# One 512-column multiplication for a unit's normalisation, and a rounding of g moved from GpSimd to ScalarE

## The chip, the core and the metric

The kernel runs on one core of a Trainium2 chip. A core has a matrix engine (TensorE: PE, with its weight loads as PEld), a vector engine (VectorE: DVE), an engine for functions and copies (ScalarE: ACT), a general engine (GpSimd: POOL) and a queue that issues transfers (SyncE: SP). Each engine works through its own list in order and waits on semaphores for the others. Time is device microseconds (us) from the first to the last instruction of one execution, with what lies around it; a kernel's time is the median of several runs.

## What is computed

Linear attention with random features, then a feed-forward layer with `h - tanh(h)`. Inputs are 8 batches, 8 heads, 576 tokens, 64 columns a head; 128 features; the second part has 4608 tokens, 512 columns in and 2048 hidden.

```python
def phi(x):
    proj = einsum('bhsd,md->bhsm', x, omega)
    h = proj - sum(x * x, -1, keepdims=True) / 2
    h = h - max(h, -1, keepdims=True)
    return exp(h) / sqrt(m)
q_p, k_p = phi(q * scale), phi(k * scale)
kv = einsum('bhsm,bhsd->bhmd', k_p, v)
z = sum(k_p, axis=2)
x = einsum('bhsm,bhmd->bhsd', q_p, kv) / (einsum('bhsm,bhm->bhs', q_p, z)[..., None] + 1e-6)
h = x @ w_in            # x as 4608 x 512
out = (h - tanh(h)) @ w_out
```

## The kernel before

Float32 precision is kept by splitting: each factor of a large product is a high part (a copy rounded to fp32r) and a low part (the factor minus its high part), and three of the four partial products are added up in PSUM: high by high, high by low, low by high.

**Attention** comes in units. A k unit (batch b, head pair c) makes the sums over keys; a q unit (chunk ch of 256 tokens, head pair c) makes the rows of x for its tokens. There are 72 q units (18 chunks by 4 pairs). The first 12, of chunks 0 to 2, run in the mode `native`, the other 60 not. A q unit that isn't native goes through these steps: load; split into `qx` (L78, L132, L133); projection on PE (L145); copy and minimum (L146, L149); exponential on ACT (L153) into `phi_q`, four blocks of 128 columns; denominators `dn` by four reductions on DVE (L350) and a reciprocal (L353); the four blocks multiplied by their `dn` (L354 to L359); four transposes on PE into `pt` (L366); split into `qh` and `ql` (L384, L385); product `pn` (L391, L392); columns put into `later` (L396 to L399). When four units of a chunk are done, `x_split` makes the chunk's `xh` and `xl` (L404, L405).

The multiplication of the four blocks asks `bank("norm")` for an engine each time. Outside `native` the list is DVE, DVE, DVE, ACT, so the first three blocks are done by DVE (L359, 128x128 each) and the last by ACT (L357).

**The feed-forward layer** goes through chunks 0 and 1 together, then chunks 2 to 5 one by one (`ffn_h`, L468 to L475, and `ffn_out`, L486 to L488), then chunks 6 to 17 in six wide blocks of two chunks, 16 steps f each. A wide step (`wide_h`) makes h for 128 hidden columns and 512 tokens by 12 matmuls (L529), tanh on ACT (L532), `g = h - tanh(h)` on DVE (L533), and then deals with the two halves of g apart. The first half is used at once: its high part `ge_w[:, 0]` by ACT (L534), its low part by DVE (L535), and six matmuls (L542 to L544, `po_w`). The second half is kept: its high part (L537) and its low part (L538), both by POOL, go into places of the weights that are no longer needed (`w`), and after the 16 steps they are the left factors of the `last` matmuls. The tile `g_w` can be written again when all four have read it.

**Order.** The program is written as interleaved generators (`tick`, `beat`), by tables of starting times, and a scheduler in the tile framework then sets the order of each engine's list by a timing model of its own, so a change of an instruction can move others. In the first 200 us of the trace chunks 0 to 2 and the decoding of weights run, until 437 us the chunks up to 5 with the attention of the next, until 870 us the wide blocks with the rest of the attention (block 0 begins around 437 us), and after that wide blocks with hardly any attention.

Of the kernel before, what the change touches and what calls it, by code (L numbers as in the profile page):

```python
# [14 lines left out]
ALU = mybir.AluOpType  # L15
AX = mybir.AxisListType

B, H, S, D, M = 8, 8, 576, 64, 128
NT, DM, DFF = B * S, H * D, 2048
P = 128  # L20
# [14 lines left out]
def favor_attention_ffn(ctx: ExitStack, tc: tile.TileContext, qT, kT, va, vt, omT, w, out):  # L35
# [12 lines left out]
    nc = tc.nc  # L48
# [18 lines left out]
    def bank(kind):  # L67
        tags = mode[kind]
        tags.append(tags.pop(0))
        return tags[-1]  # L70
# [19 lines left out]
    junk = const.tile([P, M], F32, name="junk")  # L90
# [44 lines left out]
    def features(lhs, name):  # L135

        n = len(lhs)
        ph = att("phi", [P, 4, M], F32, f"phi_{name}")
        nb = sb.tile([P, 4], F32, tag="nb", name=f"nb_{name}", bufs=12)

        for g in range(0, n, 2):
            m = min(2, n - g)
            pj = ps.tile([P, 2, 2 * M], F32, tag=bank("pj"), name=f"pj_{name}_{g}")
            for i in range(m):
                nc.tensor.matmul(pj[:, i], lhs[g + i], om2, start=True, stop=True)  # L145
            nc.scalar.copy(ph[:, g : g + m], pj[:, :m, M:])  # L146
            for i in range(m):
                j = g + i
                nc.vector.tensor_tensor_reduce(  # L149
                    ph[:, j], pj[:, i, :M], ph[:, j], scale=-SCALE, scalar=3.0e38,  # L150
                    op0=ALU.add, op1=ALU.min, accum_out=nb[:, j : j + 1])
        for j in range(n):
            nc.scalar.activation(ph[:, j], ph[:, j], AF.Exp, bias=nb[:, j : j + 1], scale=-1.0)  # L153
        return ph

    def features_f(f, toks, name):

        n = 2 * len(toks)
        ph = att("phi", [P, 4, M], F32, f"phi_{name}")
        nb = sb.tile([P, 4], F32, tag="nb", name=f"nb_{name}", bufs=12)  # L160
        pj = ps.tile([P, 4, M], F32, tag=bank("pj"), name=f"pj_{name}")
        for i, (a, b) in enumerate(toks):
            nc.tensor.matmul(pj[:, 2 * i : 2 * i + 2].rearrange("p a m -> p (a m)"), f[:, a:b],
                             om_bd.rearrange("p a m -> p (a m)"), start=True, stop=True)
        nc.vector.tensor_reduce(nb[:, :n], pj[:, :n], axis=AX.X, op=ALU.min)
        for j in range(n):
            nc.scalar.activation(ph[:, j], pj[:, j], AF.Exp, bias=nb[:, j : j + 1], scale=-1.0)
        return ph
# [150 lines left out]
    def q_unit(ch, c):  # L319
# [5 lines left out]
        while t < t0 + TC:  # L325
            e = min((t // S + 1) * S, t0 + TC)
# [3 lines left out]
        native = mode["native"]  # L330
        load(f, qT[c, :, t0 : t0 + TC])
        yield
        if native:
            ph = features_f(f, [(0, P), (P, 2 * P)], f"q{n}")
            ix = lambda h, t: 2 * t + h
        else:
# [3 lines left out]
            ph = features([x[:, h, t * P : (t + 1) * P] for h in range(2) for t in range(2)], f"q{n}")  # L340
            ix = lambda h, t: 2 * h + t
        dn = sb.tile([P, 4], F32, tag="dn", name=f"dn_{n}", bufs=8)
        for h in range(2):
            for t in range(2):
                i = ix(h, t)
                for b, s, e in pieces:
                    s, e = max(s, t * P), min(e, (t + 1) * P)
                    if s < e:
# [2 lines left out]
                            bank("junk")[r], ph[r, i], kvs[b, c][1][r, h], scale=1.0, scalar=EPS,  # L351
                            op0=ALU.mult, op1=ALU.add, accum_out=dn[r, i : i + 1])
        nc.vector.reciprocal(dn, dn)  # L353
        for i in range(4):  # L354
            e = bank("norm")
            if e is nc.scalar:
                e.mul(ph[:, i], ph[:, i], dn[:, i : i + 1])  # L357
            else:
                e.tensor_scalar(ph[:, i], ph[:, i], dn[:, i : i + 1], 1.0, op0=ALU.mult, op1=ALU.mult)  # L359
        yield  # L360
        if not native:
            yield
# [95 lines left out]
    def ffn_h(ch, s):  # L458

        p = ps.tile([P, 2, TC], F32, tag=bank("h"), name=f"h_{ch}_{s}")  # L460
        for j in range(1 if ch == 0 else 2):
            f = s if ch == 0 else 2 * s + j
            o = p if ch == 0 else p[:, j]
            r = slice(0, 2) if ch == 0 else ch % 2
            prods = [(wt[f][:, i, c * P : (c + 1) * P], x[:, r, c]) for c in range(NC)
                     for i, x in ((0, xh), (0, xl), (1, xh))]
            for i, (w_, x) in enumerate(prods):
                nc.tensor.matmul(o, w_, x, start=i == 0, stop=i == len(prods) - 1)  # L468
        g = sb.tile([P, 2, TC], F32, tag="g", name=f"g_{ch}_{s}")
        gh = sb.tile([P, 2, TC], F32R, tag="gh", name=f"gh_{ch}_{s}", bufs=2)  # L470
        gl = sb.tile([P, 2, TC], F32R, tag="gl", name=f"gl_{ch}_{s}", bufs=2)
        nc.scalar.activation(g, p, AF.Tanh)
        nc.vector.tensor_sub(g, p, g)  # L473
        nc.scalar.copy(gh, g)
        nc.vector.tensor_sub(gl, g, gh.bitcast(F32))  # L475
        return gh, gl
# [41 lines left out]
    def w_in(a, f, i, c):  # L518
        if a == 0:
            return wt[f][:, i, c * P : (c + 1) * P]  # L520
        j = TC + c % 2 * P
        return wt[2 * (f % NB) + c // 2][:, i, j : j + P]

    def wide_h(a, f):
        p = ps.tile([P, 2, TC], F32, tag=bank("h"), name=f"h_w{a}_{f}")
        prods = [(w_in(a, f, i, c), x[:, 0:2, c]) for c in range(NC)
                 for i, x in ((0, xh), (0, xl), (1, xh))]
        for i, (w_, x) in enumerate(prods):
            nc.tensor.matmul(p, w_, x, start=i == 0, stop=i == len(prods) - 1)  # L529
        g = sb.tile([P, 2, TC], F32, tag=bank("o"), name=f"g_w{a}_{f}", bufs=1 if mode["o"][-1] == "g" else 2)  # L530
        e = sb.tile([P, 2, TC], F32R, tag="gh", name=f"ge_w{a}_{f}", bufs=2)
        nc.scalar.activation(g, p, AF.Tanh)  # L532
        nc.vector.tensor_sub(g, p, g)  # L533
        nc.scalar.copy(e[:, 0], g[:, 0])  # L534
        nc.vector.tensor_sub(e[:, 1], g[:, 0], e[:, 0].bitcast(F32))  # L535
        hi, lo = [wt[f][:, i, 0:TC] for i in range(2)]
        nc.gpsimd.tensor_copy(hi, g[:, 1])  # L537
        nc.gpsimd.tensor_sub(lo, g[:, 1], hi.bitcast(F32))  # L538
        return a, f, e[:, 0], e[:, 1]

# [18 lines left out]
    def tick(new=(), force=False):  # L559
# [10 lines left out]
        chain=True, kvw=(sb, 6), zb=(sb, 6), zb0=(a0, 4), phi=(a0, 8), ph5=(a0, 2), qf=(a0, 2), qt=(a0, 2),  # L570
        kf=(a0, 3), native=True, junk=[junk, a0.tile([P, M], F32, name="junk1")],
        norm=[nc.vector,nc.scalar], o=["gl", "gh"], pj=["pj0", "pj1", "po0", "po1"], pk=["pk", "h0"],
# [26 lines left out]
    while decoded < NF:  # L599
# [24 lines left out]
    kvf.clear()  # L624
    ak = open_pool("ak")
    mode.update(
        chain=False, native=False, norm=[nc.vector, nc.vector, nc.vector, nc.scalar], junk=[junk],
        hi=nc.scalar, pj=["pj0"], pk=["pk"], pt=["pj0"],
        phi=(ak, 3), qh=(ak, 1), ql=(ak, 1), kf=(ak, 1), kx=(ak, 1), qf=(ak, 1),
        qx=(ak, 1), vr=(ak, 1), khl=(ak, 2), vhl=(ak, 2), zs=(ak, 1), c1=(ak, 1), kvs=(ak, 1))  # L630
# [44 lines left out]
    for ch in range(2, C0):  # L675
# [5 lines left out]
        for s in range(NS):  # L681
            if s > 0 and ch + 1 not in split and xdone.get(ch + 1) == NC:
                x_of(ch + 1)
            g = (ch, s, *ffn_h(ch, s))
# [30 lines left out]
    for a in range(NL):  # L715
# [3 lines left out]
        for f in range(NF):  # L719
            g = wide_h(a, f)  # L720
# [3 lines left out]
            i = NF * a + f + 6  # L724
# [7 lines left out]
        for i in range(2):  # L732
            p = ps.tile([P, DM], F32, tag=bank("h"), name=f"last_{a}_{i}")
# [44 lines left out]
```

## Time and profile before

| | |
|---|---|
| median of three runs | 1074.26 us (1074.21 to 1074.97) |
| the profiled execution | 1074.58 us |
| its span, first to last instruction | 1072.4 us |
| busy: PE, DVE, ACT, POOL | 1039.7, 857.9, 694.4, 440.2 us |
| mean granted TensorE clock | 0.995 |

A matmul of 512 columns is shown with 394 ns, but its end is modelled and the next starts some 0.23 us after it, so "busy" overstates how much PE does. A group of instructions is a line of the kernel with its engine, operation, tiles (out<-in), shape and count, then the busy time and the mean of one, then the idle time of the engine just before, with who ended it.

### The profile page before, as it was taken

The numbers are of one execution on the slowest core, as the hardware profiler recorded it, in microseconds if no ns is written. First come the engines' busy times: TensorE is split into PE (matmuls) and PEld (weight loads), VectorE is DVE, ScalarE is ACT, GpSimd is POOL, SyncE is SP. The second block draws the span as 40 slices with busy tenths as digits, with TensorE's granted clock in tenths as the row PEclk, the third lists the DMA queues.
The fourth block names the chain that finished last, engine by engine and source line by source line (L and its number), as shares of the span: only waits on it lengthen the run. The fifth ranks groups of instructions, "written<-read, shape, count | busy, mean of one in ns | idle before, by whom it ended". The sixth has DMA issues, their size and how long they took to land.

```text
span 1072.4 us, 19097 instructions
## 1 busy us (share of the span) xinstructions
PE 1039.7 (97%) x5608; PEld 887.8 (83%) x5608; DVE 857.9 (80%) x3010; ACT 694.4 (65%) x1813; POOL 440.2 (41%) x745
## 2 busy tenths in 40 slices
PE   8988999999999999999999999999999999999998
PEld 7767888988988888787888888878888888888886
DVE  6999986899999999988989988898889958742220
ACT  6997656778777777676776676667677646532220
POOL 4534541344434323555545554556355402221320
PEclk9999999999999999899999999999999999999999
DMA  8953631111111111223243332443254314332301
GB/s 281 276 172 123 251 111 56 33 34 53 33 54 36 53 38 53 82 67 91 73 126 111 114 108 91 126 130 107 63 155 124 107 42 147 113 103 85 99 0 40
DMA packets 85959, 106.17 MB, mean 99 GB/s; under 512 B 17632, under 2 KB 67936, under 8 KB 83808
## 3 DMA queue, kind: packets, MB, share of 16 engines
q1 hardware_dynamic: 85776, 104.92, 31.2%
q8 instruction: 45, 0.74, 0.3%
q14 instruction: 58, 0.48, 0.1%
q10 hardware_dynamic: 80, 0.03, 0.0%
HBM read 87.10 MB, written 17.83 MB: 98 GB/s over the span
## 4 chain that ended last, share of the span: by engine, by line
PE 55%; DVE 30%; ACT 7%; issue 5%; DMA 1%; POOL 1%; SPq 0%; DVEq 0%; POOLq 0%; ACTq 0%
PE h_w L529 15%; PE h L468 7%; DVE junk L350 4%; PE last L543 3%; PE last L544 3%; PE last L542 3%; PE po_w L544 3%; PE po_w L542 2%; PE po_w L543 2%; DVE phi_q L359 2%; PE po L486 2%; PE po L487 2%; PE po L488 2%; DVE g_w L533 2%; DVE vhl L262 2%
## 5 line engine op out<-in xcount | busy, mean ns | idle before, releaser
L529 PE MATMUL h_w<-xh,w 128*128 128x512 f32 x768 | 254.0, 394 | 2.7 <-DVE g_w L533 2.7
L529 PEld LDWEIGHTS h_w<-xh,w 128*128 128x128 f32 x768 | 143.8, 189 | 30.9 <-DVE g_w L533 4.4
L468 PE MATMUL h<-xh,w 128*128 128x256 f32 (+1 forms) x640 | 146.8, 307 | 5.0 <-DVE g L473 3.3
L529 PE MATMUL h_w<-xl,w 128*128 128x512 f32 x384 | 150.7, 393 | 0.0
L537 POOL CAST w<-g_w 128x256 fp32r<-128x256 f32 x96 | 39.7, 415 | 221.6 <-DVE g_w L533 209.5
L468 PEld LDWEIGHTS h<-xh,w 128*128 128x128 f32 x640 | 107.4, 190 | 12.5 <-DVE g L473 4.1
L350 DVE CUSTOM_DVE_ANT_0 junk<-phi_q,zb 128x128 f32<-128x128 f32 (+1 forms) x320 | 105.3, 330 | 14.8 <-ACT phi_q L153 1.0
L533 DVE TENSOR_TENSOR g_w<-h_w,g_w 128x512 f32<-128x512 f32 x96 | 65.6, 685 | 58.0 <-ACT g_w L532 57.5
L468 PE MATMUL h<-xl,w 128*128 128x256 f32 (+1 forms) x320 | 98.0, 307 | 0.3 <-DVE xl L405 0.3
L532 ACT ACTIVATE g_w<-h_w 128x512 f32<-128x512 f32 x96 | 56.6, 592 | 54.8 <-PE h_w L529 52.3
L153 ACT ACTIVATE phi_q<-phi_q,nb_q 128x128 f32<-128x128 f32 x240 | 81.0, 393 | 16.8 <-DVE nb_q L149 15.7
L529 PEld LDWEIGHTS h_w<-xl,w 128*128 128x128 f32 x384 | 72.5, 189 | 12.8
L538 POOL TENSOR_TENSOR w<-g_w,w 128x256 fp32r<-128x256 f32 x96 | 79.5, 828 | 5.1
L437 POOL TENSOR_SCALAR a<-a 128x1024 f32<-128x1024 f32 x14 | 58.4, 4173 | 52.8 <-ACT a L433 28.0
L534 ACT CAST ge_w<-g_w 128x256 fp32r<-128x256 f32 x96 | 38.9, 406 | 59.6 <-DVE g_w L533 58.5
L542 PE MATMUL po_w<-w,ge_w 128*128 128x512 f32 x192 | 75.8, 395 | 0.3 <-ACT ge_w L534 0.3
L544 PE MATMUL last<-w 128*128 128x512 f32 x192 | 75.3, 392 | 0.0
L543 PE MATMUL last<-w 128*128 128x512 f32 x192 | 75.3, 392 | 0.0
L542 PE MATMUL last<-w 128*128 128x512 f32 x192 | 75.2, 392 | 0.0
L543 PE MATMUL po_w<-w,ge_w 128*128 128x512 f32 x192 | 75.2, 392 | 0.0
L253 POOL TENSOR_TENSOR khl<-phi_ka,khl 128x256 fp32r<-128x256 f32 x48 | 37.8, 791 | 85.1 <-DVE khl L252 78.3
L544 PE MATMUL po_w<-w,ge_w 128*128 128x512 f32 x192 | 70.7, 396 | 1.2 <-DVE ge_w L535 1.2
(173 smaller groups left out, 2914.3 us busy)
## 6 DMA issues: line engine op xcount, KB each, us to landing
w<-w_in SPq DMA_DIRECT2D x320, 128.0 KB, 2.4
raw<-w SPq DMA_DIRECT2D x16, 1024.0 KB, 7.8
kf<-kT SPq DMA_DIRECT2D x32, 288.0 KB, 3.1
qf<-qT SPq DMA_DIRECT2D x72, 128.0 KB, 2.1
out<-o SPq DMA_DIRECT2D x36, 256.0 KB, 2.2
w_in<-w SPq DMA_DIRECT2D x16, 512.0 KB, 3.4
v<-vt SPq DMA_DIRECT2D x24, 288.0 KB, 2.9
v<-va SPq DMA_DIRECT2D x8, 288.0 KB, 6.0
```

The costliest lines, as they stand in the source:

```text
L153: nc.scalar.activation(ph[:, j], ph[:, j], AF.Exp, bias=nb[:, j : j + 1], scale=-1.0)
L350: nc.vector.tensor_tensor_reduce(bank("junk")[r], ph[r, i], kvs[b, c][1][r, h], scale=1.0, scalar=EPS, op0=ALU.mult, op1=ALU.add, accum_ou ...
L437: engine.tensor_scalar(a.bitcast(F32), a.bitcast(F32), 2.0**-15, 122879.9921875, op0=ALU.max, op1=ALU.min)
L468: nc.tensor.matmul(o, w_, x, start=i == 0, stop=i == len(prods) - 1)
L529: nc.tensor.matmul(p, w_, x, start=i == 0, stop=i == len(prods) - 1)
L532: nc.scalar.activation(g, p, AF.Tanh)
L533: nc.vector.tensor_sub(g, p, g)
L537: nc.gpsimd.tensor_copy(hi, g[:, 1])
L538: nc.gpsimd.tensor_sub(lo, g[:, 1], hi.bitcast(F32))
L542: nc.tensor.matmul(o, h, wt[f][:, 0, DM:], start=f == 0, stop=False)
L543: nc.tensor.matmul(o, h, wt[f][:, 1, DM:], start=False, stop=False)
L544: nc.tensor.matmul(o, l, wt[f][:, 0, DM:], start=False, stop=f == NF - 1)
```

## The change

Two edits. Outside `native` a q unit's four blocks of 128 columns are multiplied by their `dn` in one DVE instruction of 512 columns, whose second operand is `dn` repeated along each block; ACT has no part in it. And in a wide step ACT rounds the kept half of g to its high part; POOL still makes the low part. Lines behind the multiplication stand three further down in the changed kernel (L537 becomes L540).

```diff
         nc.vector.reciprocal(dn, dn)
-        for i in range(4):
-            e = bank("norm")
-            if e is nc.scalar:
-                e.mul(ph[:, i], ph[:, i], dn[:, i : i + 1])
-            else:
-                e.tensor_scalar(ph[:, i], ph[:, i], dn[:, i : i + 1], 1.0, op0=ALU.mult, op1=ALU.mult)
+        if native:
+            for i in range(4):
...
+        else:
+            nc.vector.tensor_mul(ph, ph, dn.rearrange("p (i o) -> p i o", o=1).to_broadcast([P, 4, M]))
...
         hi, lo = [wt[f][:, i, 0:TC] for i in range(2)]
-        nc.gpsimd.tensor_copy(hi, g[:, 1])
+        nc.scalar.copy(hi, g[:, 1])
         nc.gpsimd.tensor_sub(lo, g[:, 1], hi.bitcast(F32))
...
-        chain=False, native=False, norm=[nc.vector, nc.vector, nc.vector, nc.scalar], junk=[junk],
+        chain=False, native=False, junk=[junk],
```

The scheduler's lists are the same up to the first q unit that isn't native, and differ in many places after it. Three places are shown.

ACT's list in wide block 2, around the end of step 7 and step 8 (`g_w2_7` and `g_w2_8` are their g, `phi_q13_0` belongs to the q unit of chunk 13, pair 0), before:

```order
L534 CAST ge_w2_7_9257<-g_w2_7_9256 128x256
L146 COPY phi_q13_0_9215<-pj_q13_0_2_9223 128x256
L78 CAST qx_13_1_9358<-qf_13_1_9313 64x256 x2
L153 ACTIVATE phi_q13_0_9215<-phi_q13_0_9215,nb_q13_0_9216 128x128 x4
L532 ACTIVATE g_w2_8_9291<-h_w2_8_9278 128x512
L357 ACTIVATE phi_q13_0_9215<-phi_q13_0_9215,dn_13_0_9233 128x128
L301 COPY c1_6_2_9176<-pk_6_2_8928 128x256
L396 COPY later_102<-pn_12_3_9179 64x256
L397 COPY later_102<-pn_12_3_9179 64x256
L534 CAST ge_w2_8_9292<-g_w2_8_9291 128x256
```

The same place in the changed kernel:

```order
L537 CAST ge_w2_7_9134<-g_w2_7_9133 128x256
L540 CAST w7_1078<-g_w2_7_9133 128x256
L146 COPY phi_q13_0_9095<-pj_q13_0_0_9097 128x256
L153 ACTIVATE phi_q13_0_9095<-phi_q13_0_9095,nb_q13_0_9096 128x128 x2
L387 CAST qh_12_3_9022<-pt_12_3_9017 128x512
L146 COPY phi_q13_0_9095<-pj_q13_0_2_9103 128x256
L78 CAST qx_13_1_9235<-qf_13_1_9190 64x256 x2
L535 ACTIVATE g_w2_8_9168<-h_w2_8_9155 128x512
L153 ACTIVATE phi_q13_0_9095<-phi_q13_0_9095,nb_q13_0_9096 128x128 x2
L301 COPY c1_6_2_9056<-pk_6_2_8811 128x256
L537 CAST ge_w2_8_9169<-g_w2_8_9168 128x256
L540 CAST w8_1133<-g_w2_8_9168 128x256
```

The multiplication by `dn`, which stood ahead of three copies and a cast, is gone, and the rounding of the kept half follows directly on the rounding of the other half in both steps.

POOL's list around step 7 of the same block, before:

```order
L537 CAST w7_1078<-g_w2_7_9256 128x256
L293 TENSOR_TENSOR zs_6_2_8929<-zs_6_2_8929,phi_km6_2_9010 64x128
L538 TENSOR_TENSOR w7_1078<-g_w2_7_9256,w7_1078 128x256
L261 CAST vhl_6_3_0_9385<-v_6_3_9276 128x2x64
L299 TENSOR_TENSOR zhl_6_2_9173<-zs_6_2_8929,zhl_6_2_9173 128x256
```

And in the changed kernel:

```order
L293 TENSOR_TENSOR zs_6_2_8812<-zs_6_2_8812,phi_km6_2_8893 64x128
L261 CAST vhl_6_3_0_9262<-v_6_3_9153 128x2x64
L541 TENSOR_TENSOR w7_1078<-g_w2_7_9133,w7_1078 128x256
L299 TENSOR_TENSOR zhl_6_2_9053<-zs_6_2_8812,zhl_6_2_9053 128x256
L261 CAST vhl_6_3_2_9268<-v_6_3_9153 128x2x64
```

POOL's one instruction of the step now comes after the cast of `v` (L261) that it stood ahead of.

DVE's list at the passage from chunk 5 to wide block 0, around 428 us of the trace (`phi_q8_0` is a unit of chunk 8, `ql_7_3` belongs to the last unit that block 0 needs), before:

```order
L302 TENSOR_TENSOR c1_4_0_5382<-pk_4_0_5069,c1_4_0_5382 128x256
L353 RECIPROCAL dn_8_0_5478<-dn_8_0_5478 128x4
L262 TENSOR_TENSOR vhl_4_1_2_5573<-v_4_1_5418,vhl_4_1_2_5573 128x2x64
L359 TENSOR_SCALAR phi_q8_0_5460<-phi_q8_0_5460,dn_8_0_5478 128x128 x3
L385 TENSOR_TENSOR ql_7_3_5302<-pt_7_3_5296,qh_7_3_5301 128x512
```

And in the changed kernel:

```order
L302 TENSOR_TENSOR c1_4_0_5322<-pk_4_0_5012,c1_4_0_5322 128x256
L353 RECIPROCAL dn_8_0_5418<-dn_8_0_5418 128x4
L262 TENSOR_TENSOR vhl_4_1_2_5510<-v_4_1_5358,vhl_4_1_2_5510 128x2x64
L388 TENSOR_TENSOR ql_7_3_5242<-pt_7_3_5236,qh_7_3_5241 128x512
L362 TENSOR_TENSOR phi_q8_0_5400<-phi_q8_0_5400,dn_8_0_5418 128x512
```

The subtraction that makes `ql_7_3` has changed places with the normalisation of chunk 8.

## Rows read from the trace of the kernel before

**Rows 1.** The page's part 4: shares of the chain that ended last.

```profile
PE 55%; DVE 30%; ACT 7%; issue 5%; DMA 1%; POOL 1%; SPq 0%; DVEq 0%; POOLq 0%; ACTq 0%
```

**Rows 2.** Stretches: from, to and length; each engine's busy time; clock; DMA.

```profile
core 0: us, PE busy (x) PEld busy (x) DVE busy (x) ACT busy (x) POOL busy (x), PEclk, DMA share, GB/s
...
200.00:437.00 237.00, 228.28 (x1510) 206.54 (x1509) 218.77 (x878) 179.71 (x490) 93.45 (x176) 0.99 0.14 42
437.00:870.00 433.00, 427.98 (x2214) 360.10 (x2214) 387.85 (x1470) 299.05 (x824) 222.03 (x416) 1.00 0.35 106
870.00:1072.40 202.40, 198.57 (x922) 165.34 (x920) 79.20 (x250) 70.05 (x166) 40.68 (x64) 1.00 0.25 79
```

**Rows 3.** Waits of PE between 437 and 870 us: total, times, longest.

```profile
PE h_w L529 <- DVE g_w L533: 2.7, 4, 1.3
PE po_w L544 <- DVE ge_w L535: 1.2, 3, 0.8
PE po_w L542 <- ACT ge_w L534: 0.3, 1, 0.3
```

**Rows 4.** Groups of instructions between 437 and 870 us.

```profile
L538 POOL TENSOR_TENSOR w<-g_w,w 128x256 fp32r<-128x256 f32 x64 | 52.1, 815 | 2.6
...
L535 DVE TENSOR_TENSOR ge_w<-g_w,ge_w 128x256 fp32r<-128x256 f32 x64 | 36.6, 573 | 5.4 <-ACT ge_w L534 4.9
...
L359 DVE TENSOR_SCALAR phi_q<-phi_q,dn 128x128 f32<-128x128 f32 x95 | 27.0, 341 | 0.7
L537 POOL CAST w<-g_w 128x256 fp32r<-128x256 f32 x64 | 26.4, 414 | 77.9 <-DVE g_w L533 77.1
...
L534 ACT CAST ge_w<-g_w 128x256 fp32r<-128x256 f32 x64 | 25.9, 406 | 41.1 <-DVE g_w L533 40.2
...
L357 ACT ACTIVATE phi_q<-phi_q,dn 128x128 f32<-128x128 f32 x32 | 12.9, 402 | 37.2 <-DVE dn L353 37.0
```

**Rows 5.** Groups of instructions between 200 and 437 us.

```profile
L475 DVE TENSOR_TENSOR gl<-g,gh 128x512 fp32r<-128x512 f32 x29 | 23.3, 804 | 3.0 <-ACT gh L474 2.7
...
L357 ACT ACTIVATE phi_q<-phi_q,dn 128x128 f32<-128x128 f32 x19 | 7.6, 402 | 4.0 <-DVE dn L353 4.0
```

**Rows 6.** Lines L535, L475 and L359: durations, shortest, median and longest (ns).

```profile
L535 DVE TENSOR_TENSOR ge_w<-g_w,ge_w x96: 390/426/1003, 444.6 to 1045.9; 128x256 fp32r<-128x256 f32 x96
...
L475 DVE TENSOR_TENSOR gl<-g,gh x48: 660/687/1528, 92.0 to 419.9; 128x512 fp32r<-128x512 f32 x48
...
L359 DVE TENSOR_SCALAR phi_q<-phi_q,dn x204: 269/281/1060, 32.1 to 938.6; 128x128 f32<-128x128 f32 x102
```

**Rows 7.** Timeline at 428 us, DVE, then ACT, then PE.

```profile
428.53 0.68 DVE L359 TENSOR_SCALAR phi_q<-phi_q,dn 128x128 f32<-128x128 f32 x3
429.12 0.68 DVE L385 TENSOR_TENSOR ql<-pt,qh 128x512 fp32r<-128x512 f32 x1
...
428.53 0.40 ACT L357 ACTIVATE phi_q<-phi_q,dn 128x128 f32<-128x128 f32 x1 [0.40 <-DVE dn L353]
...
431.05 0.37 ACT L396 COPY later<-pn 64x256 f32<-64x256 f32 x1
...
429.86 0.39 PE L391 MATMUL pn<-qh,kvw 128*128 128x256 f32 x1 [0.78 <-DVE ql L385]
...
432.74 0.77 PE L269 MATMUL pk<-khl,vhl 128*128 128x256 f32 x2 [1.47 <-POOL khl L253]
```

**Rows 8.** Busy time in stretches of 5 us around it, columns as in rows 2.

```profile
430.00:435.00 5.00, 3.46 (x16) 3.04 (x17) 4.13 (x18) 4.05 (x13) 3.05 (x7) 0.65 0.01 3
435.00:440.00 5.00, 5.00 (x22) 4.34 (x21) 4.68 (x19) 4.36 (x12) 2.23 (x7) 0.67 0.43 130
```

**Rows 9.** Timeline at 699 us, POOL, then DVE, then PE.

```profile
699.09 1.25 POOL L538 TENSOR_TENSOR w<-g_w,w 128x256 fp32r<-128x256 f32 x1
...
699.76 1.19 DVE L133 TENSOR_TENSOR kx<-kf,kx 64x576 fp32r<-64x576 f32 x1
...
702.09 0.73 PE L544 MATMUL po_w<-w,ge_w 128*128 128x512 f32 x2 [0.82 <-DVE ge_w L535]
```

More of the change, by code (lines that the diff above doesn't have):

```diff
@@ L353, in q_unit @@
         nc.vector.reciprocal(dn, dn)
-        for i in range(4):
-            e = bank("norm")
-            if e is nc.scalar:
-                e.mul(ph[:, i], ph[:, i], dn[:, i : i + 1])
-            else:
-                e.tensor_scalar(ph[:, i], ph[:, i], dn[:, i : i + 1], 1.0, op0=ALU.mult, op1=ALU.mult)
+        if native:
+            for i in range(4):
+                e = bank("norm")
+                if e is nc.scalar:
+                    e.mul(ph[:, i], ph[:, i], dn[:, i : i + 1])
+                else:
+                    e.tensor_scalar(ph[:, i], ph[:, i], dn[:, i : i + 1], 1.0, op0=ALU.mult, op1=ALU.mult)
+        else:
+            nc.vector.tensor_mul(ph, ph, dn.rearrange("p (i o) -> p i o", o=1).to_broadcast([P, 4, M]))
         yield
```

## The prediction, made before the changed kernel ran

> **What bounds the kernel now.** I read the chain of waits first, then busy time by stage, then who makes PE wait, then the groups of the lines that the change touches, and last the timeline at two places. The chain runs through PE for 55%, DVE for 30% and ACT for 7% [rows 1]. By stage, PE is busy all but 8.7 us of the 237 us from 200 to 437, all but 5.0 us of the 433 us of the wide blocks with attention, and all but 3.8 us of the last 202 us [rows 2]. DVE is second: 92% of the first of these stretches (218.77 of 237), 90% of the second (387.85 of 433), 39% of the last. So the kernel is bound by PE, and what can be won at all is where DVE's list, nearly full, makes PE wait. There is not much: the visible gaps are about 14 us in both stretches together, and one loss that isn't idle time: at 430 to 440 us the granted clock was 0.65 and 0.67 [rows 8], between 1.2 and 2.4 GHz on average, where PE stood idle for 0.78 and 1.47 us in short succession [rows 7]. That dip cost 0.35 x 5 + 0.33 x 5 = 3.4 us of full-speed PE.
>
> In the wide blocks the waits of PE are for DVE's two operations of a step, 2.7 us for g (L533) and 1.2 us for its low part (L535), and 0.3 us for ACT's rounding [rows 3]. Nothing there waits for POOL's L537 or L538, whose results are needed only after the block.
>
> **The multiplication, on DVE.** 60 units each lose three instructions of 128 columns and gain one of 512. Undisturbed, the three take 0.68 us from the first's start to the last's end, since the next starts while the one before is still ending, and a 512-column subtraction of DVE right behind takes 0.68 us too [rows 7]. So undisturbed the edit saves DVE nothing: four blocks now cost what three did, and the fourth is ACT's saving. Disturbed, the three cost 3 x (341 - 281) = 0.18 us more on average [rows 4, 6]; the nearest 512-column operation with both inputs in SBUF, L475, averages 804 ns where its median is 687, so 0.12 us more [rows 5, 6]. No row has an operand that is repeated along a block, as `dn` is now. The bounds are 60 x (0.12 - 0.18) = -3.6 us of DVE time, and 60 x 0.12 = +7.2 us if the new one is disturbed where the old ones were not; 30% of each on the chain is -1.1 to +2.2 us. I take **0**: the median rows are equal. The four transposes behind it now all wait for one end where the first could start after a third of it; the end is the same.
>
> The Trainium skill (VectorE: DVE Perf Modes, section The perf-mode tier table) says that float32 `tensor_scalar` in SBUF runs at twice the rate of `tensor_tensor`, which speaks against this edit: at the page's 0.96 GHz, 512 elements one by one against 384 two by two would be an estimated 0.33 us more a unit. The trace doesn't show that difference: 0.68 us against 0.68 us.
>
> **ACT.** It loses 60 multiplications (402 ns) and gains 96 casts, which I price at the identical shape that it does already, 406 ns [rows 4]. From 200 to 437 us that is only a gain: 19 instructions, 7.6 us, and the 4.0 us in which ACT stood at them waiting for the reciprocal [rows 5]. From 437 to 870 us it is 12.9 us less and 64 x 0.406 = 26.0 us more, a net 13.1 us; ACT goes from 299 to some 312 us of 433 and stays far from full. The cast adds no wait of its own: it waits for the same g as L534, and the order shows it directly behind L534. What queues behind it are copies of projections, exponentials and the next tanh, on which DVE waits. With ACT's 7% of the chain: +0.9 us for the net 13.1; -0.8 for the 11.6 us of the first stretch. In the second, 37.0 us of ACT's standing at L357 go as well [rows 4], with copies of `c1` and `later` behind it in the list; 7% is -2.6, of which I take half, -1.3, because what comes next often needs the same DVE. Sum **-1.2 us**; the bounds are -3.4 (relief whole, casts hidden) and +26 (each cast on the path).
>
> **POOL.** It loses 26.4 us (L537) in the second stretch. That time was idle cover anyway, POOL being half busy; what matters is DVE. L535 has a median of 426 ns and a longest of 1003 [rows 6], a mean of 573 in the stretch [rows 4]: 64 x 0.147 = 9.4 us of being held. One such chain is to be seen whole at 699 us: L538 runs for 1.25 us, DVE's L133 beside it for 1.19, L535 comes late and PE stands 0.82 us [rows 9]. Now L538 can't start until ACT has done two casts, 0.81 us after g, by which time an L535 that came promptly is nearly over. I take half of the 9.4 us as saved, and 30% of that for the chain: **-1.4 us**. The bounds are 0 and the waits of rows 3 whole, -4.2. On the other side L538 ends some 0.4 us later after g, and POOL's `khl` behind it with it; POOL is 1% of the chain [rows 1], so I cost that at nothing.
>
> The Trainium skill (SBUF — State Buffer, section Who interferes with whom) says that whichever of a GpSimd instruction and a DVE instruction with two SBUF inputs starts first holds the shared ports to its end. The stretched L133 agrees. By it L538's holding is not removed but moved on to whatever DVE does 0.4 us later, and this term could be 0.
>
> **The passage to block 0.** Here the order shows a real change: `ql_7_3` (L385) now precedes the multiplication, so it starts about 0.59 us earlier (428.53 for 429.12), and PE's wait of 0.78 us for it shrinks to about 0.2 [rows 7]. ACT loses L357 there (0.40 us, after a 0.40 us wait), so `later` (L396) comes earlier too. I take 0.6 + 0.4 = **-1.0 us**, and leave the clock as it was.
>
> **Sum.** 0 - 1.2 - 1.4 - 1.0 = -3.6 us. The profiled execution took 1074.58 us, so 1070.98; it stood 0.32 us over the median, which gives 1070.7 us. The last 202 us I cost at nothing: DVE and ACT have room there.
>
> **Rivals.**
>
> *No difference.* What is freed lies where PE sets the pace, or what held DVE holds it elsewhere; the passage alone remains. 1074.3 - 1.0 = 1073.3 us. For it: PE at 97 to 99% busy, and DVE's own work unchanged. Against: PE's waits in the wide blocks are for exactly those DVE operations.
>
> *Clock kept.* If the passage loses enough idle time, the clock doesn't fall at 431 us: 3.4 us more, 1067.3 us. For: two of its three gaps sit behind lists that moved (the third is `khl`, 1.47 us, and PE has transposes to do before it now). Against: the projections and short matmuls there remain.
>
> *Slower, through ACT.* Each cast delays what stands behind it by 0.406 us, 64 times in the second stretch. If the chain runs through ACT in a share s of the steps, the sum becomes -4.5 + 26 s; slower than the bound at s over a quarter, and at 0.4 it is +5.9, or 1080.2 us. For: ACT waits 40.2 us at L534 for g [rows 4], so it often arrives early and the cast then pushes all behind it. Against: ACT's 7% of the chain, and those very idle times as slack.
>
> *The multiplication is dearer.* If it takes L475's 804 ns against 680, DVE gets 7.2 us more and the time is 2.2 us above the forecast, 1072.9 us; that is within no difference. By the page's rates it would be 20 us of DVE and, at 30%, some 1077 us; rows 7 leave that little room.
>
> **Chances.** A measurement of this kernel tells about 0.2% (2.1 us) from no change, so faster means below 1072.1 us and slower above 1076.4. Forecast 0.46 (its own range 1068.5 to 1072.1); clock kept 0.15; no difference 0.25, with the dearer multiplication at 804 ns in it; slower 0.14, of which 0.02 for a multiplication at the page's rates. That makes faster 0.61, same 0.25, slower 0.14. The range goes from 1066.0, a little under the case of the kept clock for ACT's and POOL's better bounds, to 1077.0, leaving out most of the slower case.
>
> **What would show it.** Right: the new multiplication near 0.69 us when undisturbed; DVE's busy time within 10 us of before; L535's mean well under 573 ns; the cast at 406 ns; PE's waits for L533 and L535 below 3.9 us; L391's wait at the passage gone or small. Wrong: PE waits that end with ACT lines (L146, L532, L534), DVE idle time before L149 or L398 that grows by more than a few us; the L535 mean unchanged with other DVE lines stretched by L538; a second stretch at a low clock. An order that opens a new gap at a block's start, which no row of before can price, would make all of this wrong in either direction.

## The result, and the profile after

The changed kernel took 1079.40 us (median of 4 runs, 1078.47 to 1080.20) against 1074.62 us for the kernel before beside it: a ratio of 1.0044, 95% interval 1.0027 to 1.0061. The forecast was 1070.7 us, so the sign was wrong: 4.8 us slower instead of 3.6 us faster. The profiled execution took 1079.24 us, with a span of 1077.5 us against 1072.4.

In the code after, every line behind the first edit stands three lower: the cast `hi` is L540 (ScalarE now), the subtraction `lo` L541, `g` L536, the copy `ge` L537, its low part L538, and the new multiplication is L362.

Busy time (share of the span, instructions) and the chain that ended last, to be held against [rows 1]:

```profile
PE 1040.2 (97%) x5608; PEld 885.5 (82%) x5608; DVE 857.8 (80%) x2890; ACT 702.6 (65%) x1849; POOL 402.6 (37%) x649
...
PE 60%; DVE 27%; ACT 6%; issue 4%; POOL 2%; DMA 1%; DVEq 0%; SPq 0%; POOLq 0%; ACTq 0%
```

VectorE's work is the same to a tenth of a microsecond (857.9 before), GpSimd lost 37.6 us and ScalarE gained 8.2. Nothing became a bound by its amount of work. Against [rows 2]:

```profile
200.00:437.00 237.00, 227.40 (x1512) 204.49 (x1511) 219.22 (x830) 170.64 (x467) 91.40 (x169) 1.00 0.14 42
437.00:870.00 433.00, 423.79 (x2191) 355.49 (x2192) 382.67 (x1398) 306.48 (x851) 203.54 (x360) 1.00 0.35 104
...
870.00:1077.50 207.50, 203.68 (x949) 169.65 (x947) 84.90 (x256) 80.63 (x199) 24.74 (x32) 1.00 0.25 80
```

In the second row PE stands idle for 9.2 us where it was 5.0. Who makes it wait there, against [rows 3] (total us, times, longest):

```profile
PE h_w L532 <- DVE g_w L536: 4.6, 7, 1.0
PE po_w L547 <- DVE ge_w L538: 1.3, 2, 0.7
PE h_w L532 <- DVE xl L408: 0.8, 1, 0.8
PE pj_q L145 <- ACT g_w L535: 0.6, 1, 0.6
PE pt L369 <- DVE later L402: 0.6, 1, 0.6
PE pk L269 <- POOL khl L253: 0.6, 1, 0.6
```

The wait for `g` rose from 2.7 to 4.6 us, and four partners appear that were not in [rows 3]. The groups of the touched lines in the same stretch, against [rows 4]:

```profile
L541 POOL TENSOR_TENSOR w<-g_w,w 128x256 fp32r<-128x256 f32 x64 | 53.1, 832 | 76.3 <-ACT w L540 62.4 <-DVE nb_q L149 5.0 <-DVE dn L353 3.4
...
L538 DVE TENSOR_TENSOR ge_w<-g_w,ge_w 128x256 fp32r<-128x256 f32 x64 | 38.5, 603 | 5.1 <-ACT ge_w L537 4.4
...
L537 ACT CAST ge_w<-g_w 128x256 fp32r<-128x256 f32 x64 | 26.0, 407 | 42.7 <-DVE g_w L536 42.1
L540 ACT CAST w<-g_w 128x256 fp32r<-128x256 f32 x64 | 25.8, 403 | 1.4 <-DVE g_w L536 1.4
L362 DVE TENSOR_TENSOR phi_q<-phi_q,dn 128x512 f32<-128x512 f32 x31 | 24.5, 791 | 0.7
```

VectorE's subtraction for the low part (L538) was to become quicker than its 573 ns and became slower, 603. And at the passage to block 0, against [rows 7, 8], first the timeline, then two stretches of 5 us:

```profile
431.58 0.68 DVE L388 TENSOR_TENSOR ql<-pt,qh 128x512 fp32r<-128x512 f32 x1
432.18 0.68 DVE L362 TENSOR_TENSOR phi_q<-phi_q,dn 128x512 f32<-128x512 f32 x1
...
432.32 0.39 PE L394 MATMUL pn<-qh,kvw 128*128 128x256 f32 x1 [0.18 <-DVE ql L388]
```

```profile
430.00:435.00 5.00, 2.56 (x14) 1.65 (x13) 4.67 (x23) 3.13 (x11) 0.32 (x2) 1.00 0.23 76
435.00:440.00 5.00, 4.21 (x24) 3.10 (x23) 4.91 (x18) 4.60 (x15) 4.64 (x11) 1.00 0.11 35
```

Here the order did what the prediction read from it: the wait of 0.78 us is 0.18, and the granted clock stays at 1.00 where it was 0.65 and 0.67. So the condition of the rival *clock kept* was met, and the kernel is slower all the same.

### The profile page after: what moved, and what is told of

It reads as the page before. It is cut to its first block, busy times and chain, and to the rows that moved or that the text cites. A ratio compares the mean times of both kernels' runs of the same rounds, so it can differ in the third digit from the quotient of the medians.

```text
span 1077.5 us, 18913 instructions
## 1 busy us (share of the span) xinstructions
PE 1040.2 (97%) x5608; PEld 885.5 (82%) x5608; DVE 857.8 (80%) x2890; ACT 702.6 (65%) x1849; POOL 402.6 (37%) x649
## 4 chain that ended last, share of the span: by engine, by line
PE 60%; DVE 27%; ACT 6%; issue 4%; POOL 2%; DMA 1%; DVEq 0%; SPq 0%; POOLq 0%; ACTq 0%
PE h_w L532 16%; PE h L471 8%; PE last L545 4%; PE last L547 4%; PE last L546 4%; DVE junk L350 4%; PE po_w L547 3%; PE po_w L546 3%; PE po_w L545 3%; PE po L489 2%; PE po L490 2%; PE po L491 2%; DVE g_w L536 2%; PE pj_q L145 2%; DVE vhl L262 1%
## 5 line engine op out<-in xcount | busy, mean ns | idle before, releaser
L532 PE MATMUL h_w<-xh,w 128*128 128x512 f32 x768 | 250.5, 392 | 4.6 <-DVE g_w L536 4.6
L541 POOL TENSOR_TENSOR w<-g_w,w 128x256 fp32r<-128x256 f32 x96 | 77.8, 812 | 237.8 <-ACT w L540 212.0
L350 DVE CUSTOM_DVE_ANT_0 junk<-phi_q,zb 128x128 f32<-128x128 f32 (+1 forms) x320 | 103.1, 324 | 14.4 <-ACT phi_q L153 1.7
L536 DVE TENSOR_TENSOR g_w<-h_w,g_w 128x512 f32<-128x512 f32 x96 | 65.7, 686 | 55.1 <-ACT g_w L535 54.5
L153 ACT ACTIVATE phi_q<-phi_q,nb_q 128x128 f32<-128x128 f32 x240 | 82.3, 394 | 17.5 <-DVE nb_q L149 16.7
L535 ACT ACTIVATE g_w<-h_w 128x512 f32<-128x512 f32 x96 | 56.6, 593 | 52.6 <-PE h_w L532 48.9
L537 ACT CAST ge_w<-g_w 128x256 fp32r<-128x256 f32 x96 | 39.1, 407 | 67.5 <-DVE g_w L536 66.7
L538 DVE TENSOR_TENSOR ge_w<-g_w,ge_w 128x256 fp32r<-128x256 f32 x96 | 54.7, 571 | 15.9 <-ACT ge_w L537 15.0
```

What stands on the lines that cost most here:

```text
L350: nc.vector.tensor_tensor_reduce(bank("junk")[r], ph[r, i], kvs[b, c][1][r, h], scale=1.0, scalar=EPS, op0=ALU.mult, op1=ALU.add, accum_ou ...
```

## The experiments

Two questions were open after this: whether the two edits cost time as operations, or the scheduler's newly written lists do; and, if an edit does, through which engine. In the kernels whose lists are marked *of before* in the table, each engine's list of the kernel before is held fixed by a chain of order-only dependencies that is added at the kernel's end; in norm_new_order it is the list of the changed kernel. Only the named edit then differs.

```diff
+    for row in ORDER:                      # one list for each engine
...
+            if last is not None:
+                tc.add_manual_dep(ins[at], last.name, info, reason="order")
+            last = ins[at]
```

All ratios are to the kernel before on the same chip. The last three columns are us by which the profiled execution falls behind the profiled one of before: up to 98 us (the start), from there to 448 us (narrow chunks and the passage), and from there to the end. They are read from the start times of the same products of the up-projections, and are single executions. Where the lists differ, the last two columns depend on where the line is drawn: by the columns that have gone through PE, the changed kernel lies 2.7 us behind at 448 us, 1.1 at 500, 0.3 at 600 and 5.2 at 870, of which 1.1 are the start each time.

| kernel | operations | lists | ratio (95%) | start | to 448 | to the end |
|---|---|---|---|---|---|---|
| after | both edits | its own | 1.0044 (1.0027, 1.0061) | 1.1 | 1.6 | 2.4 |
| both_old_order | both edits | of before | 1.0028 (1.0017, 1.0040) | 1.4 | 0.5 | 2.3 |
| norm_new_order | multiplication | of after | 1.0013 (1.0003, 1.0022) | -0.5 | 1.1 | -0.5 |
| norm_only | multiplication | its own | 1.0051 (1.0038, 1.0064) | 1.2 | 1.6 | 3.9 |
| hi_only | hi on ScalarE | its own | 0.9991 (0.9982, 0.9999) | 1.3 | 0.2 | -1.1 |
| hi_old_order | hi on ScalarE | of before | 1.0022 (1.0013, 1.0031) | 0.3 | -0.2 | 3.3 |
| norm_old_order | multiplication | of before | 0.9990 (0.9981, 0.9998) | 0.4 | 0.1 | -1.2 |
| old_shift_a | as before | redrawn | 1.0035 (1.0022, 1.0047) | 1.3 | 1.5 | 0.9 |
| old_shift_b | as before | redrawn | 0.9992 (0.9983, 1.0001) | 1.4 | 2.4 | -1.8 |
| act_extra | + work on ScalarE | of before | 1.0030 (1.0018, 1.0043) | 2.0 | 0.0 | 3.6 |
| pool_short | - work on GpSimd | of before | 0.9975 (0.9964, 0.9986) | 0.5 | 0.1 | -1.8 |
| lo_late | hi on ScalarE, lo later | of before but lo | 1.0053 (1.0041, 1.0066) | 2.1 | 0.2 | 5.5 |
| hi_late | hi on ScalarE, later | of before but hi | 1.0026 (1.0017, 1.0035) | 0.5 | 0.1 | 3.1 |
| new_shift_a | both edits | redrawn | 1.0004 (0.9995, 1.0013) | 1.2 | 1.1 | -0.7 |
| new_shift_b | both edits | redrawn | 1.0008 (0.9999, 1.0017) | 0.7 | -1.5 | 2.9 |

### Operations or lists

Both edits in the lists of before, and the changed kernel's lists with GpSimd making `hi` again, directly ahead of `lo`:

> Both edits, but every engine's list is held to the order of the kernel before: the 512-column multiplication stands where the first of the three DVE multiplications stood, ACT's rounding of the kept half directly behind its rounding of the other half, and everything else as it was. Theory 'operations': ACT's 64 casts in the wide blocks with attention delay what DVE waits for, and the time is that of the changed kernel, 1077 to 1080 us. Theory 'lists': the operations are neutral or a small gain, as the prediction summed them, and the loss comes with the new lists that the scheduler made; then 1070 to 1075 us.

> The changed kernel's lists, but GpSimd makes the high part again, directly ahead of its low part in GpSimd's list; the 512-column multiplication stays. Theory 'operations': without ACT's casts the loss goes, 1072 to 1075 us. Theory 'lists': the lists are those of the changed kernel, so 1077 to 1080 us.

Then each edit alone, with the scheduler free:

> The 512-column multiplication alone, GpSimd makes the high part, the scheduler free to order. Theory 'operations': no ACT casts, so 1073 to 1075 us. Theory 'lists': a new order is drawn, and the time can lie anywhere from 1070 to 1081 us; nothing is said of the side.

> ACT's rounding of the kept half alone, the multiplication by the four separate instructions as before, the scheduler free to order. Theory 'operations': all of the loss, 1078 to 1081 us, or a little more since ACT keeps its 60 multiplications. Theory 'lists': a new order is drawn, anywhere from 1070 to 1081 us.

Measured: 1.0028, 1.0013, 1.0051, 0.9991. Neither theory fits all four. In fixed lists `hi` costs: taking it back in the lists of after brings 1.0044 to 1.0013. With the scheduler free it costs nothing (0.9991), and then the multiplication, which no list held fixed charges much for, is the slow one (1.0051). So each edit was also tried alone in the lists of before:

```diff
-        nc.gpsimd.tensor_copy(hi, g[:, 1])
+        nc.scalar.copy(hi, g[:, 1])
```

> The kernel before with one edit: ScalarE makes hi, right behind the copy of g's first half, and every engine's list is otherwise held to the order of the kernel before. Operations theory (ScalarE's cast delays what VectorE and TensorE wait for, whatever the order): of the 2.7 us that both edits cost in these lists (1.0028 of before) nearly all is this edit's, since taking it back in the changed kernel's lists gave about 3.3 us outside the start: 1.0020 to 1.0030 of before, the waits of h_w for g_w longer. Lists theory (both edits are neutral, the new lists lose): 0.998 to 1.001. Redraw theory (an edit of a fraction of a microsecond moves every later meeting of the engines, with either sign): anything between 0.998 and 1.003, and no simple sum with the other edit.

```diff
+            nc.vector.tensor_mul(ph, ph, dn.rearrange("p (i o) -> p i o", o=1).to_broadcast([P, 4, M]))
```

> The kernel before with the other edit: one multiplication of 512 columns at the place of the first of the four, every engine's list otherwise held to the order of the kernel before. Operations theory: the multiplication lasts as long as the three small ones together, so 0.999 to 1.001 of before. Lists theory: the same. Late-tile theory (the first transposes of a unit now wait for all four columns at once, and TensorE meets them sooner than VectorE ends): 1.001 to 1.003, with more waits of the transposes of phi_q on VectorE's multiplication. If this edit and the one of hi each cost 1 to 1.5 us, the 2.7 us of both in these lists are their plain sum.

Measured: `hi` 1.0022, the multiplication 0.9990. Three pairs share their lists and differ by `hi` alone: before to hi_old_order +0.22%, norm_old_order to both_old_order +0.38%, norm_new_order to after +0.31%. That is 2.4 to 4.1 us. Two pairs differ by the multiplication alone: -0.10% (before to norm_old_order) and +0.06% (hi_old_order to both_old_order). So the multiplication is neutral as an operation and `hi` is not.

### How much a redrawn list is worth

One number in the table of starts, and no operation, is changed, in the kernel before and in the changed one:

```diff
-                k = [(28,31,34,37),(43,46,49,52),(40,55,58,64),(61,70,76,82),(67,73,79,85)][ch - 3][c]
+                k = [(29,31,34,37),(43,46,49,52),(40,55,58,64),(61,70,76,82),(67,73,79,85)][ch - 3][c]
```

(the `_b` kernels turn 40 into 41 instead)

> The kernel before with no operation changed: one number in the table of starts, the first unit of the first wide chunk from 28 to 29, so that the scheduler writes other lists. Operations theory: the lists are of the same quality, so within 0.1% of before (0.999 to 1.001). Redraw theory: the time moves by 2 to 5 us, with either sign (0.995 to 1.005), which would be as much as the changed kernel lost.

> The kernel before with no operation changed: one other number in the table of starts, the first unit of the third wide chunk from 40 to 41. Operations theory: 0.999 to 1.001 of before. Redraw theory: 0.995 to 1.005, another value than that of the other shifted start. If both come out slower and neither faster, the lists of the kernel before are a picked draw: a change that redraws them pays some microseconds whatever it does.

> The changed kernel with no operation changed: the first unit of the first wide chunk starts at 29 instead of 28, so the scheduler writes other lists. If the changed kernel's own lists are an unlucky draw, this one comes out 1 to 4 us faster than it: 1.000 to 1.0035 of before. If the change itself asks for worse lists, 1.004 to 1.006.

> The changed kernel with no operation changed: the first unit of the third wide chunk starts at 41 instead of 40. Unlucky draw: 1.000 to 1.0035 of before, and another value than that of the other shifted start. Trait of the change: 1.004 to 1.006. With the operations alone at 1.0028 (both edits in the lists of the kernel before), draws on either side of that would say that the lists add spread and no cost of their own.

Measured: 1.0035 and 0.9992 around the kernel before, 1.0004 and 1.0008 around the changed one at 1.0044. The same operations span 0.4% by the draw of the lists, as much as the change was measured to cost. The changed kernel stands at the dear end of its own draws; what its lists lose beyond the other two is not a trait of the change. The three draws of before (1, 1.0035, 0.9992) average 1.0009 and those of the changed kernel 1.0019: with the scheduler free, these runs show no cost of the change that stands out from the spread.

### Through which engine `hi` costs

ScalarE's extra time and GpSimd's relief are now taken apart, both in the lists of before:

```diff
-        nc.scalar.copy(e[:, 0], g[:, 0])
+        nc.scalar.copy(e[:, 0], g[:, 0]); nc.scalar.copy(spare, g[:, 1, 0:16]); nc.scalar.copy(spare, g[:, 1, 16:32])
```

> The kernel before in its own lists, GpSimd keeping its cast of hi; ScalarE gets two more casts of 16 columns right behind the copy of g's first half, into a spare tile that nobody reads (together about as long as one of 256 columns, which left no room for a tile). ScalarE's-queue theory (the 0.4 us of the cast delay what stands behind it on ScalarE, and VectorE behind that): nearly the whole +2.4 us of the moved hi in these lists, 1.0015 to 1.003 of before. GpSimd's-subtraction theory (the cast costs ScalarE nothing that matters; it is lo, started a cast later, that meets VectorE's subtraction and holds up GpSimd's list): 0.999 to 1.001.

```diff
-        nc.gpsimd.tensor_copy(hi, g[:, 1])
+        nc.gpsimd.tensor_copy(hi[:, 0:16], g[:, 1, 0:16])
```

> The kernel before in its own lists, GpSimd's cast of hi cut from 256 to 16 columns (the other 240 columns of hi are left out: they keep the old weights, and lo is taken against those); ScalarE gets nothing. So GpSimd is relieved and nothing is added elsewhere. My prediction's term for VectorE's relief: 0.997 to 0.999 (some 1.4 us and more). GpSimd's-subtraction theory: the cast never held VectorE, and lo now starts earlier beside VectorE's subtraction of e, so VectorE's subtractions beside lo grow in number and the time is 0.999 to 1.001.

Measured: 1.0030 and 0.9975. The groups from 437 to 870 us that show the two edits, ScalarE's of act_extra, then GpSimd's of pool_short:

```profile
L534 ACT CAST spare<-g_w 128x16 fp32r<-128x16 f32 x128 | 25.9, 202 | 2.0
```

```profile
L537 POOL CAST w<-g_w 128x16 fp32r<-128x16 f32 x64 | 13.8, 217 | 80.0 <-DVE g_w L533 79.3
```

Two casts of 202 ns (25.9 us in the stretch, as the cast of 256 columns takes) cost 3.2 us with GpSimd untouched. ScalarE's-queue theory holds, GpSimd's-subtraction theory as the main cause falls. The relief of 0.2 us a step on GpSimd alone is worth 2.7 us, but not at the place where the prediction looked for it, VectorE's subtraction L535, whose mean was 573 ns before and is, in pool_short,

```profile
L535 DVE TENSOR_TENSOR ge_w<-g_w,ge_w 128x256 fp32r<-128x256 f32 x64 | 36.8, 575 | 5.4 <-ACT ge_w L534 4.9
```

The two effects' sum, +0.05%, is below the +0.22% of the moved `hi`, but the intervals (0.09 to 0.13% to either side each) don't settle whether the rest is real. What could be in it is that `lo` now waits for ScalarE.

VectorE's list is the same in these kernels, instruction for instruction, so its delay between 440 and 868 us can be split into longer waits and longer instructions. Act_extra falls 3.7 us behind there: waits that end with ScalarE grow by 1.6 us, waits that end with GpSimd by 0.9, and instructions by 1.1. Hi_old_order falls 3.7 us behind as well: 1.6, 0.8 and 1.5 (the rest are smaller waits and others). Pool_short gains 1.6 us: its instructions are 2.8 us shorter, and its waits 1.2 us longer. So the same cast time on ScalarE costs VectorE the same waits whether it is `hi` or work that nobody reads.

Two kernels moved one of the two steps in its list:

> ScalarE makes hi in the lists of the kernel before (1.0022 of before as it stood), but GpSimd's subtraction lo is moved behind the next item of GpSimd's list, in 56 of 96 places (in the others the next item is another lo). GpSimd's-subtraction theory (GpSimd stood waiting for ScalarE's cast with urgent work behind it): most of the 2.4 us come back, 0.999 to 1.0012. ScalarE's-queue theory: nothing comes back, 1.0015 to 1.003.

> ScalarE makes hi in the lists of the kernel before, but two places later in ScalarE's list, behind the next two items; GpSimd's list keeps lo in its place. ScalarE's-queue theory (the items right behind the cast are the ones that are late): a good part of the 2.4 us comes back, 0.999 to 1.0015. GpSimd's-subtraction theory: GpSimd waits for hi still longer, so 1.002 to 1.006.

Measured: 1.0053 and 1.0026; nothing came back in either. GpSimd's groups of lo_late, and then of hi_late, in the same stretch:

```profile
L538 POOL TENSOR_TENSOR w<-g_w,w 128x256 fp32r<-128x256 f32 x64 | 50.4, 787 | 30.2 <-ACT w L537 30.1
...
L253 POOL TENSOR_TENSOR khl<-phi_ka,khl 128x256 fp32r<-128x256 f32 x28 | 21.9, 783 | 69.8 <-DVE khl L252 52.8 <-PE h_w L529 7.5 <-PE pk L307 5.3
```

```profile
L538 POOL TENSOR_TENSOR w<-g_w,w 128x256 fp32r<-128x256 f32 x64 | 52.0, 813 | 123.9 <-ACT w L537 102.7 <-DVE ge_w L535 6.7 <-DVE phi_q L359 4.5
```

In lo_late GpSimd no longer stands for the cast (30.1 us instead of the 76.2 us of hi_old_order) but stands in front of `khl` instead, with `lo` queued behind it. In hi_late the cast's later place makes GpSimd wait 102.7 us for it. Lo_late misses both expectations: nothing came back, where GpSimd's-subtraction theory expected most of it, and 1.0053 lies above the 1.0015 to 1.003 of ScalarE's-queue theory, so a later `lo` has a price of its own. Hi_late missed what ScalarE's-queue theory expected of it: either the items right behind the cast are not the only ones that pay, or what was freed there was lost at GpSimd. This pair doesn't tell which; neither shift finds `hi` a cheaper place.

### One place seen whole

The cast delays what stands right behind it in ScalarE's list, and at some steps VectorE then waits. The kernel before at 457 to 463 us, ScalarE's rounding, exponential (L153) and copy of a projection (L146), and VectorE's readers of these two, L252 and L149:

```profile
457.19 0.41 ACT L534 CAST ge_w<-g_w 128x256 fp32r<-128x256 f32 x1 [0.37 <-DVE g_w L533]
457.51 1.28 ACT L153 ACTIVATE phi_ka<-phi_ka,nb_ka 128x128 f32<-128x128 f32 x4
...
462.12 0.41 ACT L534 CAST ge_w<-g_w 128x256 fp32r<-128x256 f32 x1 [1.02 <-DVE g_w L533]
462.44 0.36 ACT L146 COPY phi_q<-pj_q 128x256 f32<-128x256 f32 x1
...
458.65 0.48 DVE L252 CAST khl<-phi_ka 128x256 fp32r<-128x256 f32 x2
...
462.90 0.28 DVE L149 CUSTOM_DVE_ANT_0 phi_q<-pj_q,phi_q 128x128 f32<-128x128 f32 x1
```

The same place in hi_old_order, some 0.5 to 1 us later:

```profile
457.64 0.41 ACT L534 CAST ge_w<-g_w 128x256 fp32r<-128x256 f32 x1 [0.36 <-DVE g_w L533]
457.95 0.40 ACT L537 CAST w<-g_w 128x256 fp32r<-128x256 f32 x1
458.26 1.28 ACT L153 ACTIVATE phi_ka<-phi_ka,nb_ka 128x128 f32<-128x128 f32 x4
...
462.83 0.41 ACT L534 CAST ge_w<-g_w 128x256 fp32r<-128x256 f32 x1 [0.98 <-DVE g_w L533]
463.15 0.40 ACT L537 CAST w<-g_w 128x256 fp32r<-128x256 f32 x1
463.45 0.36 ACT L146 COPY phi_q<-pj_q 128x256 f32<-128x256 f32 x1
...
458.98 0.88 DVE L252 CAST khl<-phi_ka 128x256 fp32r<-128x256 f32 x2 [0.20 <-ACT phi_ka L153]
...
463.85 0.29 DVE L149 CUSTOM_DVE_ANT_0 phi_q<-pj_q,phi_q 128x128 f32<-128x128 f32 x1 [0.15 <-ACT phi_q L146]
```

And VectorE's two readers in act_extra:

```profile
461.18 0.74 DVE L252 CAST khl<-phi_ka 128x256 fp32r<-128x256 f32 x1 [0.23 <-ACT phi_ka L153]
...
465.94 0.29 DVE L149 CUSTOM_DVE_ANT_0 phi_q<-pj_q,phi_q 128x128 f32<-128x128 f32 x1 [0.19 <-ACT phi_q L146]
```

Before, the exponential and the copy start 0.32 us after the rounding L534; in hi_old_order 0.62 us after it, with the cast `hi` between. VectorE waits 0.20 us for the exponential and 0.15 us for the copy where it waited for neither; in act_extra, 0.23 and 0.19 us. At the next two steps, around 468 and 473 us, the same delay costs nothing: two exponentials, then a copy, start 0.3 us late behind the cast, and VectorE gets to them only later.

PE loses that time only later, at 475 us, where it comes to a projection (`pj_q`) that needs VectorE's L149. Before, and then in hi_old_order:

```profile
473.07 0.41 ACT L534 CAST ge_w<-g_w 128x256 fp32r<-128x256 f32 x1 [0.63 <-DVE g_w L533]
...
473.58 0.74 POOL L538 TENSOR_TENSOR w<-g_w,w 128x256 fp32r<-128x256 f32 x1
...
474.04 0.56 DVE L535 TENSOR_TENSOR ge_w<-g_w,ge_w 128x256 fp32r<-128x256 f32 x1
...
475.29 0.48 PE L145 MATMUL pj_q<-om,qx 128*128 128x256 f32 x2
```

```profile
474.18 0.41 ACT L534 CAST ge_w<-g_w 128x256 fp32r<-128x256 f32 x1 [0.61 <-DVE g_w L533]
...
474.97 0.74 POOL L538 TENSOR_TENSOR w<-g_w,w 128x256 fp32r<-128x256 f32 x1 [1.70 <-ACT w L537]
...
475.14 0.84 DVE L535 TENSOR_TENSOR ge_w<-g_w,ge_w 128x256 fp32r<-128x256 f32 x1
...
476.68 0.48 PE L145 MATMUL pj_q<-om,qx 128*128 128x256 f32 x2 [0.79 <-DVE nb_kb L149]
```

PE stands 0.79 us where it stood for nothing. Against the kernel before, VectorE's list had by then fallen 0.7 us further back than PE's, and at this step it loses another 0.3: its subtraction L535 starts while `lo` is running, which here starts 0.79 us after L534 instead of 0.51, and takes 0.84 us instead of 0.56. In act_extra PE waits 0.51 us at the same matmul, although L535 takes 0.56 us there as before: that is the delay of the earlier steps alone.

Most steps show no such loss. From step to step of the wide blocks (95 differences to the kernel before), five of act_extra lost 0.3 us or more, 2.6 us of 3.5 in all, and five of hi_old_order 3.2 us, of which two others won 0.7 back.

## Why the prediction was wrong, step by step

**The multiplication (0 us): right as an operation.** In fixed lists it gave -1.1 and +0.6 us, inside the bounds of -1.1 and +2.2. L362's mean in the wide blocks lies 0.10 us above its median of 691 ns; L475 had suggested 0.12, and the three short ones had 0.18 together [rows 4, 5, 6]. VectorE's busy time agrees within 0.1 us.

**ScalarE (-1.2 us): the step that failed.** The price was right, 403 ns against 406, and the place was right, directly behind L534. What failed is its worth: the prediction priced both what ScalarE gains and what it loses at its 7% share of the chain, and called its idle time slack. By edit, that gave `hi` 7% of 26.0 us less the 1.4 us of GpSimd's relief, +0.4 us, and the multiplication -0.8, -0.9 (7% of 12.9 us) and -1.3, or -3.0 us. In fixed lists `hi` cost 2.4 to 4.1 us and the multiplication -1.1 and +0.6. Act_extra measures the share itself: 25.9 us of casts in the wide blocks with attention cost 3.2 us, 12% of them (those of the 32 steps after 870 us cost nothing). Where ScalarE is relieved of L357 as well, the moved `hi` cost no less (+0.38%, norm_old_order to both_old_order). The 60 multiplications and the 37.0 us of standing at L357, for which the prediction took -0.8 and -1.3 us, went in norm_old_order too, and that kernel as a whole gained 1.1 us with VectorE's part in it. Idle time ahead of L534 [rows 4] was not slack for what stands behind the cast: ScalarE waits there for VectorE's g, so the step starts with both casts still to do, and the exponentials and copies that VectorE needs come behind them. At some steps VectorE has other work meanwhile, and at a few it waits.

**GpSimd and L535 (-1.4 us): wrong in its mechanism.** Cutting the cast on GpSimd alone gained 2.7 us, but L535 was held no less by it (10.0 us against 9.8); the time came from VectorE's other instructions. The prediction let VectorE's held time at L535 vanish by half, and it grew. Counted from the records of both lines between 437 and 870 us, with held time as duration over 420 ns: before, 7 of 64 of VectorE's subtractions began while `lo` was running (mean 746 ns, 2.3 us held), and all 64 were held for 9.8 us; after, 17 began so (mean 795 ns, 6.4 us), and all were held for 11.7 us. In hi_old_order it is 13 and 11.4 us. Nor does the held time of L535 go with the time of the kernel: it was least, 8.5 us, in lo_late, the slowest kernel of all, and 12.0 us in hi_only, one of the fastest. `Lo` starts a cast later after g, and a subtraction that comes late, as many do, meets it. The sentence on the Trainium skill's page (SBUF — State Buffer, section Who interferes with whom), that whichever of the two starts first holds the shared ports to its end, agrees: in all 24 cases (7 before, 17 after) L535 ended 279 to 285 ns after `lo` had ended, however late in `lo` it had started, and with no GpSimd work beside it L535 took 421 ns. The prediction used the rule to doubt the term and not to reverse it. The half microsecond by which `lo` and `khl` end later, costed at nothing, is not settled: VectorE's waits for GpSimd grew by 0.8 us in hi_old_order, but by 0.9 us in act_extra too, where GpSimd kept its cast.

**The passage (-1.0 us, clock as it was): right on the wait, too low on the clock.** The wait went from 0.78 to 0.18 us and the clock didn't fall. That gain can't be found again in the time: without the start the changed kernel lies 1.6 us behind at 448 us, level at 500, 0.8 us ahead at 600, and 4.1 us behind at 870. Ahead of the passage other gaps had opened. PE's waits between 200 and 444 us, of which these are the largest after,

```profile
PE pk L305 <- DVE c L302: 2.0, 3, 1.3
PE h L471 <- DVE g L476: 1.8, 2, 1.1
PE pk L269 <- issue: 1.1, 2, 0.8
```

add up to 10.8 us against 8.4 before, and none of the three was there at that size. That is the sentence at the prediction's end, an order that opens new gaps; it was named and given no chance, and it should have had one. New_shift_b, with the same operations, gained 1.5 us in the same stretch although its granted clock was 0.70 from 430 to 435 us. The last 202 us, which the prediction costed at nothing, cost nothing: 5.2 us behind at 870, 5.1 at the end.

**The rivals.** *Slower, through ACT* was worked out as 1080.2 us, and 1079.4 was measured; that the two lie so near is luck. It needed 40% of the casts' time on the path and the whole relief; measured were 12% and a relief that came to little. The chance of 0.14 was too small mostly for the draw of the lists, which no case had. *Clock kept* came true in its condition and gave 4.8 us slower.

What stands: with the lists held, `hi` on ScalarE costs about 3 us (2.4 to 4.1 us in three pairs, one of them in lists that were written for it, norm_new_order to after), and the rest lies within the spread of redrawn lists. What stays open: fixed lists keep the order but not the timing, so that each of these few microseconds may itself hold some of that spread; and the one kernel whose scheduler answered the cast alone with lists of its own, hi_only, shows 0.9991, by a better answer or by the luck of its draw. No version that computes everything beats the kernel before by more than 0.1%: norm_old_order (1074.91 us) and hi_only (1074.16 us) are the two whose intervals lie below 1.

## What to carry to other kernels

Work handed from an engine with room to another one with room is priced by what stands behind it in the new engine's list, above all where that engine starts each step late on a wait: its idle time ahead of the step isn't slack. A step at which two engines hold each other up isn't removed by moving its neighbour; look at which instruction will lie beside it then. And where a change makes a scheduler write new lists, shift a harmless number first, with no operation changed: that spread (0.4% here) is the least that the range of a prediction must hold, and a change smaller than it is judged in fixed lists.

## What the runs showed of the hardware that was not expected

The first 30 us differ between executions by up to 2 us with the same instructions in the same order, most of it before 12 us. Before and after between 5 and 10 us (PE busy, and its instructions in parentheses; the clock is third from the end), and the first eight matmuls of that stretch in each:

```profile
5.00:10.00 5.00, 4.17 (x21) 3.63 (x22) 2.17 (x4) 2.23 (x9) 2.48 (x11) 1.00 1.04 294
...
5.45 2.00 PE L163 MATMUL pj_k<-om_bd,kf 128*128 128x256 f32 x8 [0.62 <-POOL om_bd L112]
```

```profile
5.00:10.00 5.00, 4.54 (x14) 3.75 (x15) 1.38 (x2) 1.14 (x4) 2.49 (x11) 1.00 1.08 292
...
5.46 3.78 PE L163 MATMUL pj_k<-om_bd,kf 128*128 128x256 f32 x8 [0.63 <-POOL om_bd L112]
```

The same eight matmuls took 2.00 us in one execution and 3.78 in the other, nearly twice as long, while the granted clock's row says 1.00 in both. There is nothing between: 1.99 or 2.00 us in seven of the sixteen profiled executions and 3.78 in nine. The nine are the ones with 1.1 to 2.1 us in the column of the start; the others lie between -0.5 and 0.7 of the kernel before. What decides it stays open. A comparison of two profiled executions has to take the start off first: of the 5.1 us between the spans of before and after, 1.1 lie there.
